# Spectral filter and feed-forward on one core: the inverse transform over d with cosine and sine planes for half of the positions

## The chip, the cores and the metric

The kernel runs on one core of a Trainium2 chip. TensorE (PE in the profile) multiplies, VectorE (DVE) and ScalarE (ACT) work elementwise, GpSimd (POOL) does small things, and SyncE (SP), ACT and POOL issue the transfers (DMA). The metric is the device time of one execution in microseconds; three executions before the change took 1285.08, 1282.17 and 1284.58 us, the median is 1284.58.

## The reference

The input x has 2048 positions of 1024 values. After a layer norm it goes two ways: a two-dimensional real Fourier transform, a pointwise filter and the transform back; and a feed-forward network with 3584 hidden values. Their product is added to x.

```python
xn = _layernorm(x)
X = rfft2(xn, axes=(-2, -1))          # 2048 x 513
s = irfft2(X * (w_r + 1j * w_i), s=(2048, 1024), axes=(-2, -1))
h = silu(einsum("bsd,df->bsf", xn, w1))
g = silu(einsum("bsf,fd->bsd", h, w2))
return x + s * g
```

Only the last step of `irfft2`, the one that goes from 513 frequencies over d to 1024 positions, is touched by the change.

## The kernel before

Every operand of a matmul is split into a high and a low half in float16, and each product is made of three matmuls (high x high, high x low, low x high) that accumulate in float32 in PSUM.

The program is one list of matmuls with other work woven into it. First comes the first layer of the network (`mm1`, tiles pa, line 421), with the layer norm and the forward transform in between. Then comes the second layer: it is computed by seven block products m = 0 to 6 instead of eight (a Strassen scheme over two halves of the rows and of the columns), each with eight row blocks j = 0 to 7 of 42 matmuls of 512 columns (`mm2`, tiles pb, lines 499 to 501). A row block is evacuated by `acc`; its weights `w` are read as `jr`, split by ACT and DVE (lines 216 and 219) in the product before, and its left operands `ht` are loaded on ACT's queue two row blocks ahead (lines 1386 to 1388). Products 4 to 6 also finish output tiles: they read the spectral result back (`fs`) and x (`fx`), multiply, add and store.

The filter (`f_gen`) and the inverse transform (`i_gen`) are background jobs. After every half row block `work` lets them take steps. A meter (lines 175 to 186) adds up an estimated cost for each instruction on PE and on DVE; a background step is taken only while DVE's sum is not more than LEAD = 1.0 ahead of PE's (line 1285). Each job also yields a number of steps of its own.

`i_gen` runs once for each of four column classes c, in the order 1, 3, 0, 2. The four tiles iu (`mat`, line 1121) transform over the positions s; `post` and `split` on ACT and DVE turn them into the operands us, one for each group g of frequencies over d (group 0 holds the residues 0 and 4 modulo 8, group g the residues g and 8 - g). Then for each of four blocks p of 128 rows:

- `mat2(p)` (line 1150) makes one PSUM tile id of four groups x 256 columns. In each group the columns are two planes of 128 positions. It takes 24 matmuls of 256 columns: four groups, three terms, and r = 0 (real part) and 1 (imaginary part). Each has a weight load of 128 x 128 of its own.
- `bfly(p)` copies half of id to SBUF on ACT (line 1156), and on DVE forms sums and differences of groups 0 and 2 and of 1 and 3 (lines 1161 to 1164, 256 elements each), then the eight output pieces of 128 positions with ten operations of 128 elements (lines 1169 to 1178). The tile s is stored to sd by a transfer on SP's queue (line 1189), to be read back as fs.

The PSUM tiles iu and id come from a pool with two buffers (tag ft), the tiles pb from one with four. In SBUF, tags uc, ub, ud and so have one buffer each, s has two. A matmul that writes into a PSUM buffer waits until ACT and DVE have read what was there before; ACT, DVE and each DMA queue take their instructions in the order in which the program issues them.

Of the kernel before, what the change touches and what calls it, by code (L numbers as in the profile page):

```python
# [10 lines left out]
F32 = mybir.dt.float32  # L11
I32 = mybir.dt.int32
AF = mybir.ActivationFunctionType
OP = mybir.AluOpType
# [19 lines left out]
RH = math.sqrt(0.5)  # L34
# [3 lines left out]
def _halves(v, scale):  # L38
    v = v * scale
    hi = v.astype(np.float16)  # L40
    return hi, (v - hi.astype(np.float64)).astype(np.float16)


def make_constants():

    d0 = np.arange(128)[:, None, None]
    d1 = np.arange(8)[None, :, None]
    k1 = np.arange(64)[None, None, :]
    th = 2 * np.pi * (((8 * d0 + d1) * k1) % 1024) / 1024
# [12 lines left out]
    kc = np.stack(_halves(k, 2.0**14), 3)  # L62

    ci = np.zeros((128, 4, 2, 256))
    idx = np.arange(64)[:, None]
    dd = np.arange(128)[None, :]
    alt = np.where(dd[0] % 2 == 0, 1.0, -1.0)
    for g in range(4):
        for h, cl in enumerate((0, 4) if g == 0 else (g, 8 - g)):
            kd = 8 * idx + cl  # L70
            ph = 2 * np.pi * ((kd * dd) % 1024) / 1024
            co, si = 2 * np.cos(ph), 2 * np.sin(ph)
            r = slice(64 * h, 64 * h + 64)
            sg = 1 if h == 0 else -1
            if g == 0:
                ci[r, g, 0] = np.concatenate([co, sg * co], 1)
                ci[r, g, 1] = np.concatenate([-si, -sg * si], 1)
            else:
                ci[r, g, 0] = np.concatenate([co, sg * si], 1)
                ci[r, g, 1] = np.concatenate([-si, sg * co], 1)  # L80
    ci[0, 0, 0] = 1.0
    ci[0, 0, 1] = np.concatenate([alt, alt])
# [12 lines left out]


def spectral_ffn(ctx, tc, x, w_r, w_i, w1, w2, ca, kc, ci, tw, pm, out):
    nc = tc.nc
# [14 lines left out]
    pt = ctx.enter_context(tc.tile_pool(name="pt", bufs=2, space=PSUM))  # L113
# [23 lines left out]
    def defer(n, fn):  # L137
        deferred.append([n, fn])
# [53 lines left out]
    def radix4(sign, b, d, o):  # L192

        sub = nc.vector.tensor_tensor
        plus, minus = ((2, 7), (6, 3)) if sign < 0 else ((6, 3), (2, 7))

        def pick(i):
            st = i[1] - i[0]
            stop = i[1] + (1 if st > 0 else -1)
            return o[:, i[0]:stop:st]  # L200

        sw = d[:, 1, ::-1]
        sub(o[:, 0:2], b[:, 0], b[:, 1], op=OP.add)
        sub(o[:, 4:6], b[:, 0], b[:, 1], op=OP.subtract)
        sub(pick(plus), d[:, 0], sw, op=OP.add)
        sub(pick(minus), d[:, 0], sw, op=OP.subtract)
# [880 lines left out]
    C = {}  # L1087
# [16 lines left out]
    def i_gen(c):  # L1104
        ip = C["p"]
        tt, stt = nc.vector.tensor_tensor, nc.vector.scalar_tensor_tensor
# [17 lines left out]
        def post(g):  # L1124
            ps = psu.pop(g)
            cpy = ip.tile([128, 2, 256], F32, name=f"uc{c}_{g}", tag="uc", bufs=1)
            nc.scalar.activation(cpy, ps[:, 2:4], AF.Copy)
            b = ip.tile([128, 2, 2, 128], F32, name=f"ub{c}_{g}", tag="ub", bufs=1)
            d = ip.tile([128, 2, 2, 128], F32, name=f"ud{c}_{g}", tag="ud", bufs=1)
            tt(b.rearrange("m c r k -> m c (r k)"), ps[:, 0:2], cpy, op=OP.add)  # L1130
            tt(d.rearrange("m c r k -> m c (r k)"), ps[:, 0:2], cpy, op=OP.subtract)
# [11 lines left out]
        psd = {}  # L1143

        def mat2(p):
            ps = pt.tile([128, 2, 2, 256], F32, name=f"id{c}_{p}", tag="ft")
            for g, o in ((0, ps[:, 0, 0]), (2, ps[:, 0, 1]), (1, ps[:, 1, 0]), (3, ps[:, 1, 1])):
                for n, (uh, ch) in enumerate(((0, 0), (0, 1), (1, 0))):
                    for r in range(2):
                        nc.tensor.matmul(o, us[g][:, uh, 2 * p + r], C["ci"][:, ch, g, r], start=(n == 0 and r == 0), stop=(n == 2 and r == 1))  # L1150
            psd[p] = ps

        def bfly(p):
            ps = psd.pop(p)
            cpy = ip.tile([128, 2, 256], F32, name=f"sc{c}_{p}", tag="uc", bufs=1)
            nc.scalar.activation(cpy, ps[:, :, 1], AF.Copy)
            pq = ip.tile([128, 2, 2, 128], F32, name=f"spq{c}_{p}", tag="ub", bufs=1)
            ab = ip.tile([128, 2, 2, 128], F32, name=f"sab{c}_{p}", tag="ud", bufs=1)
            pqf = pq.rearrange("s n r k -> s n (r k)")
            abf = ab.rearrange("s n r k -> s n (r k)")  # L1160
            tt(pqf[:, 0], ps[:, 0, 0], cpy[:, 0], op=OP.add)
            tt(abf[:, 0], ps[:, 1, 0], cpy[:, 1], op=OP.add)
            tt(pqf[:, 1], ps[:, 0, 0], cpy[:, 0], op=OP.subtract)
            tt(abf[:, 1], ps[:, 1, 0], cpy[:, 1], op=OP.subtract)
            pc, qp, pm_, qm = pq[:, 0, 0], pq[:, 0, 1], pq[:, 1, 0], pq[:, 1, 1]
            u, t_, r, v = ab[:, 0, 0], ab[:, 0, 1], ab[:, 1, 0], ab[:, 1, 1]
# [3 lines left out]
            tt(o12[:, 1], r, t_, op=OP.add)  # L1170
            tt(s_[:, 0], pc, u, op=OP.add)
            tt(s_[:, 4], pc, u, op=OP.subtract)
            tt(s_[:, 2], pm_, v, op=OP.subtract)
            tt(s_[:, 6], pm_, v, op=OP.add)
            stt(s_[:, 1], o12[:, 0], RH, qm, op0=OP.mult, op1=OP.add)
            stt(s_[:, 5], o12[:, 0], -RH, qm, op0=OP.mult, op1=OP.add)
            stt(s_[:, 7], o12[:, 1], RH, qp, op0=OP.mult, op1=OP.add)
            stt(s_[:, 3], o12[:, 1], -RH, qp, op0=OP.mult, op1=OP.add)
# [71 lines left out]
    with tc.manual_schedule():  # L1250
# [134 lines left out]
        for n, (m, j) in enumerate(seq):  # L1385
# [15 lines left out]
            ps = pf.tile([128, 512], F32, name=f"pb{m}_{j}", tag="ff")  # L1401
# [52 lines left out]
```

## Time and profile before

| | |
|---|---|
| three timed runs | 1285.08, 1282.17, 1284.58 us |
| span of the profiled execution | 1282.3 us; the page has no other time for this execution |
| PE, DVE, ACT, POOL busy | 1261.7, 951.1, 464.5, 120.1 us |
| id matmuls (line 1150) | 384, first at 934.8, last at 1153.0 us |
| iu matmuls (line 1121) | 384, 43.2 us busy |
| pb matmuls (lines 499 to 501) | 3 x 798, 299.5 to 299.7 us busy for each line |
| read from and written to HBM | 189.06 and 104.33 MB |

A row of the groups reads: line, engine, operation, output <- inputs, shape, count | busy time, mean of one in ns | idle time of the engine just before, and what ended it. A row of the timeline reads: start, duration (us), engine, line, operation, count. A row of the windows reads: the stretch, its length, then busy time and count for PE, weight loads, DVE, ACT and POOL, then the granted clock, the share of the DMA engines and GB/s. A row of the waits reads: who waited <- for whom: total, number, longest.

### The profile page before, as it was taken

The numbers are of one execution on the slowest core, as the hardware profiler recorded it, in microseconds if no ns is written. First come the engines' busy times: TensorE is split into PE (matmuls) and PEld (weight loads), VectorE is DVE, ScalarE is ACT, GpSimd is POOL, SyncE is SP. The second block draws the span as 40 slices with busy tenths as digits, with TensorE's granted clock in tenths as the row PEclk, the third lists the DMA queues.
The fourth block names the chain that finished last, engine by engine and source line by source line (L and its number), as shares of the span: only waits on it lengthen the run. The fifth ranks groups of instructions, "written<-read, shape, count | busy, mean of one in ns | idle before, by whom it ended". The sixth has DMA issues, their size and how long they took to land.

```text
span 1282.3 us, 18847 instructions
## 1 busy us (share of the span) xinstructions
PE 1261.7 (98%) x6991; PEld 656.3 (51%) x6991; DVE 951.1 (74%) x1856; ACT 464.5 (36%) x572; POOL 120.1 (9%) x241
## 2 busy tenths in 40 slices
PE   8999999999999999999999998999999999999997
PEld 5545445444544544445455554544555556564444
DVE  7688988899879897978587998872564657685344
ACT  4864443434455555535242221211322223233111
POOL 2220000002000000012101111132001010000000
PEclk9999999999999999999999998999999999999999
DMA  7585667546676997589789899969597799869894
GB/s 248 131 186 153 167 192 235 168 126 189 215 236 207 288 281 227 171 277 240 184 241 290 216 266 233 280 215 317 127 310 196 277 300 318 288 214 320 267 360 165
DMA packets 267373, 298.86 MB, mean 233 GB/s; under 512 B 38928, under 2 KB 193296, under 8 KB 266640
## 3 DMA queue, kind: packets, MB, share of 16 engines
q1 hardware_dynamic: 247408, 238.85, 62.7%
q10 hardware_dynamic: 15840, 51.45, 11.6%
q0 software_dynamic: 4032, 7.34, 3.5%
q8 instruction: 55, 0.90, 0.3%
q14 instruction: 38, 0.31, 0.1%
HBM read 189.06 MB, written 104.33 MB: 229 GB/s over the span
## 4 chain that ended last, share of the span: by engine, by line
PE 84%; DMA 7%; DVE 4%; SPq 1%; issue 1%; ACT 1%; POOL 0%; ACTq 0%; DVEq 0%; POOLq 0%
PE pa L421 40%; PE pb L499 11%; PE pb L500 11%; PE pb L501 11%; PE id L1150 3%; PE iu L1121 3%; DMA vq<-vd 2%; DMA jr<-ws 1%; SPq L453 1%; PE fx L903 1%; DMA kq<-in_kc_dram 1%; DMA hd_dif<-hoone 1%; ACT xp L658 1%; DMA hd_sum<-hosum 1%; DVE w L219 1%
## 5 line engine op out<-in xcount | busy, mean ns | idle before, releaser
L421 PE MATMUL pa<-xnT,w 128*128 128x512 f16 x2688 | 585.0, 379 | 1.1 <-ACT w L216 0.7
L421 PEld LDWEIGHTS <-w 128*128 128x128 f16 x2688 | 262.1, 98 | 311.9 <-DVE w L219 1.3
L499 PE MATMUL pb<-w,ht 128*128 128x512 f16 (+1 forms) x798 | 299.7, 376 | 0.0
L500 PE MATMUL pb<-w,ht 128*128 128x512 f16 (+1 forms) x798 | 299.5, 375 | 0.0
L501 PE MATMUL pb<-w,ht 128*128 128x512 f16 (+1 forms) x798 | 299.5, 375 | 0.0
L501 PEld LDWEIGHTS <-ht 128*128 128x128 f16 x798 | 78.2, 98 | 91.3 <-issue 0.3
L499 PEld LDWEIGHTS <-ht 128*128 128x128 f16 x798 | 78.2, 98 | 87.9
L500 PEld LDWEIGHTS <-ht 128*128 128x128 f16 x798 | 78.2, 98 | 87.8
L430 ACT ACTIVATE h<-pa,s 128x512 f32<-128x512 f32 x112 | 75.7, 678 | 129.2 <-PE pa L421 117.2
L216 ACT ACTIVATE w<-jr,sc 128x512 f16<-128x512 f32 x98 | 68.4, 713 | 85.6 <-PE pb L501 31.6
L219 DVE SCALAR_TENSOR_TENSOR hoone<-h,hs,hoone 128x2048 f16<-128x2048 f32 x28 | 65.7, 2346 | 18.5 <-ACT hoone L216 18.5
L219 DVE SCALAR_TENSOR_TENSOR w<-jr,sc,w 128x512 f16<-128x512 f32 x98 | 71.7, 749 | 2.0 <-ACT w L216 2.0
L216 ACT ACTIVATE hoone<-h,hs 128x2048 f16<-128x2048 f32 x28 | 55.9, 1998 | 45.3 <-DVE h L464 23.7
L216 ACT ACTIVATE hosum<-hr,hs 128x1536 f16<-128x1536 f32 x28 | 44.0, 1573 | 55.3 <-DVE hr L460 34.3
L930 ACT ACTIVATE zq<-Z,zs 128x1024 f16<-128x1024 f32 x16 | 18.3, 1146 | 104.4 <-DVE Z L1003 57.3
L903 PE MATMUL fx<-vq,kq 128*128 128x256 f16 x192 | 45.5, 281 | 7.8 <-DMA vq<-vd 7.8
L219 DVE SCALAR_TENSOR_TENSOR hosum<-hr,hs,hosum 128x1536 f16<-128x1536 f32 x28 | 50.8, 1814 | 2.5 <-ACT hosum L216 2.5
L459 DVE TENSOR_TENSOR hr<-h 128x1024 f32<-128x1024 f32 x28 | 34.2, 1222 | 21.7 <-ACT h L430 21.5
L216 ACT ACTIVATE w<-w1r,rs 128x1024 f16<-128x1024 f32 x28 | 31.9, 1144 | 47.0 <-DVE w L219 31.8
L580 ACT ACTIVATE pl<-pl,c 128x512 f32<-128x512 f32 (+1 forms) x26 | 16.9, 682 | 82.3 <-DVE pl L559 53.6
L239 DVE TENSOR_REDUCE m<-w1r 128x1 f32<-128x1024 f32 x28 | 33.8, 1211 | 16.1 <-DMA w1r<-in_B_w_dram 16.1
L1150 PE MATMUL id<-cis,us 128*128 128x256 f16 x384 | 43.2, 273 | 0.0
(188 smaller groups left out, 1534.7 us busy)
## 6 DMA issues: line engine op xcount, KB each, us to landing
w1r<-in_B_w_dram SPq DMA_DIRECT2D x28, 512.0 KB, 6.1
hd_sum<-hosum SPq DMA_DIRECT2D x56, 256.0 KB, 2.9
hd_one<-hoone SPq DMA_DIRECT2D x56, 256.0 KB, 3.7
hd_dif<-hoone SPq DMA_DIRECT2D x56, 256.0 KB, 3.2
w2m<-in_B_w_dram SPq DMA_DIRECT2D x28, 512.0 KB, 5.4
ht<-hd_dif ACTq DMA_DIRECT2D x32, 448.0 KB, 8.3
jr<-in_B_w_dram SPq DMA_DIRECT2D x56, 256.0 KB, 6.1
ht<-hd_sum ACTq DMA_DIRECT2D x32, 448.0 KB, 5.3
```

Of the source, the lines that this page charges most:

```text
L216: nc.scalar.activation(hi, raw, AF.Copy, scale=scale)
L219: nc.vector.scalar_tensor_tensor(lo, raw, scale, hi, op0=OP.mult, op1=OP.subtract)
L239: nc.vector.tensor_reduce(m1[:, i:i + 1], raw[i], axis=AX.XY, op=OP.max, apply_absolute_value=True)
L421: nc.tensor.matmul(ps, w[:, wh, d], xt[:, xh, d], start=(n == 0), stop=(n == 23))
L430: nc.scalar.activation(hq[:, 2 * (c % 2) + f % 2], ps, AF.Silu, scale=s1[:, f:f + 1])
L459: tt(sums[:, 0:2], hq[:, 0::2], hq[:, 1::2], op=OP.subtract)
L499: nc.tensor.matmul(ps, hh[:, 0], w[:, 0], start=first, stop=False)
L500: nc.tensor.matmul(ps, hh[:, 0], w[:, 1], start=False, stop=False)
L501: nc.tensor.matmul(ps, hh[:, 1], w[:, 0], start=False, stop=last)
L903: nc.tensor.matmul(o, k[:, c, kh, 1], v[:, c, vh], start=(n == 0), stop=False)
L1121: nc.tensor.matmul(ps[:, q], lhs, rhs, start=(n == 0 and r == 0), stop=(n == 2 and r == 1))
L1150: nc.tensor.matmul(o, us[g][:, uh, 2 * p + r], C["ci"][:, ch, g, r], start=(n == 0 and r == 0), stop=(n == 2 and r == 1))
```

## The change

A cosine is the same at positions d and 128 - d, a sine has the opposite sign. The constants ci no longer hold two full planes of 128 positions, but for each plane the positions below 64 in order or 63 down to 1, the cosines (r = 0, columns 0 to 129) apart from the sines (r = 1, columns 127 or 130 to 255). Columns 127 to 129 hold the positions 64 and 0 that have no partner. `mat2` keeps its 24 matmuls for a tile, but those of r = 0 have 130 columns, those of r = 1 have 129 in groups 1 to 3 and 256 in group 0; the groups now follow in the order 0, 1, 2, 3. In `bfly`, ACT copies the sine columns (504 elements) and two sets of 8 single positions; DVE forms near - sine and near + sine for 63 positions of every plane (two operations of 504 elements, the second written backwards), then sums and differences of groups 0 and 2, 1 and 3 (two operations of 512), and the same ten operations of 128 with outputs in two runs of 64. The tile pa is new; dm takes the buffer of the copy (uc), o12 a part of kk (ub). In `post`, the tiles b and d become one tile.

```diff
-    dd = np.arange(128)[None, :]
+    dd = np.arange(65)[None, :]
+    up, down = slice(1, 64), slice(63, 0, -1)
...
+            re, im = ci[r, g, 0], ci[r, g, 1]
+            re[:, 0:64], re[:, 127] = co[:, 0:64], co[:, 64]
+            im[:, 127], im[:, 130:193] = si[:, 64], si[:, up]
             if g == 0:
-                ci[r, g, 0] = np.concatenate([co, sg * co], 1)
-                ci[r, g, 1] = np.concatenate([-si, -sg * si], 1)
+                re[:, 64:127], re[:, 128], re[:, 129] = sg * co[:, down], sg * co[:, 64], sg * co[:, 0]
+                im[:, 128], im[:, 193:256] = sg * si[:, 64], -sg * si[:, down]
             else:
-                ci[r, g, 0] = np.concatenate([co, sg * si], 1)
-                ci[r, g, 1] = np.concatenate([-si, sg * co], 1)
+                re[:, 64:127], re[:, 128] = sg * si[:, down], sg * si[:, 64]
+                im[:, 128], im[:, 129], im[:, 193:256] = -sg * co[:, 64], sg * co[:, 0], sg * co[:, down]
...
         def mat2(p):
-            ps = pt.tile([128, 2, 2, 256], F32, name=f"id{c}_{p}", tag="ft")
-            for g, o in ((0, ps[:, 0, 0]), (2, ps[:, 0, 1]), (1, ps[:, 1, 0]), (3, ps[:, 1, 1])):
-                for n, (uh, ch) in enumerate(((0, 0), (0, 1), (1, 0))):
-                    for r in range(2):
-                        nc.tensor.matmul(o, us[g][:, uh, 2 * p + r], C["ci"][:, ch, g, r], start=(n == 0 and r == 0), stop=(n == 2 and r == 1))
+            ps = pt.tile([128, 4, 256], F32, name=f"id{c}_{p}", tag="ft")
+            for g in range(4):
+                for r, cols in enumerate((slice(0, 130), slice(0 if g == 0 else 127, 256))):
+                    for n, (uh, ch) in enumerate(((0, 0), (0, 1), (1, 0))):
+                        nc.tensor.matmul(
+                            ps[:, g, cols], us[g][:, uh, 2 * p + r], C["ci"][:, ch, g, r, cols],
+                            start=(r == 0 and n == 0), stop=(r == 1 and n == 2), skip_group_check=True)
...
         def bfly(p):
-            cpy = ip.tile([128, 2, 256], F32, name=f"sc{c}_{p}", tag="uc", bufs=1)
-            nc.scalar.activation(cpy, ps[:, :, 1], AF.Copy)
-            pq = ip.tile([128, 2, 2, 128], F32, name=f"spq{c}_{p}", tag="ub", bufs=1)
-            ab = ip.tile([128, 2, 2, 128], F32, name=f"sab{c}_{p}", tag="ud", bufs=1)
...
-            tt(pqf[:, 0], ps[:, 0, 0], cpy[:, 0], op=OP.add)
-            tt(abf[:, 0], ps[:, 1, 0], cpy[:, 1], op=OP.add)
-            tt(pqf[:, 1], ps[:, 0, 0], cpy[:, 0], op=OP.subtract)
-            tt(abf[:, 1], ps[:, 1, 0], cpy[:, 1], op=OP.subtract)
+            cpy = ip.tile([128, 4, 2, 63], F32, name=f"sc{c}_{p}", tag="uc", bufs=1)
+            kk = ip.tile([128, 4, 4, 64], F32, name=f"sk{c}_{p}", tag="ub", bufs=1)
+            nc.scalar.activation(cpy.rearrange("s g k d -> s g (k d)"), ps[:, :, 130:256], AF.Copy)
+            nc.scalar.activation(kk[:, :, 0:2, 0], ps[:, :, 0:128:127], AF.Copy)
+            nc.scalar.activation(kk[:, :, 2:4, 0], ps[:, :, 129:127:-1], AF.Copy)
+            near = ps[:, :, 1:127].rearrange("s g (k d) -> s g k d", k=2)
+            tt(kk[:, :, 0::3, 1:64], near, cpy, op=OP.subtract)
+            tt(kk[:, :, 1:3, 63:0:-1], near, cpy, op=OP.add)
+            pa = ip.tile([128, 2, 2, 128], F32, name=f"spa{c}_{p}", tag="pa", bufs=1)
+            dm = ip.tile([128, 2, 2, 128], F32, name=f"sdm{c}_{p}", tag="uc", bufs=1)
+            tt(pa.rearrange("s g k d -> s (g k d)"), kf[:, 0:512], kf[:, 512:1024], op=OP.add)
+            tt(dm.rearrange("s g k d -> s (g k d)"), kf[:, 0:512], kf[:, 512:1024], op=OP.subtract)
...
-            o12 = ip.tile([128, 2, 128], F32, name=f"so{c}_{p}", tag="so", bufs=1)
+            o12 = kf[:, 0:256].rearrange("s (n d) -> s n d", n=2)
...
-            tt(s_[:, 0], pc, u, op=OP.add)
+            tt(both(0), pair(pc), pair(u), op=OP.add)
...
-            stt(s_[:, 1], o12[:, 0], RH, qm, op0=OP.mult, op1=OP.add)
+            stt(both(1), pair(o12[:, 0]), RH, pair(qm), op0=OP.mult, op1=OP.add)
...
```

`both(j)` is the pair of runs of 64 positions, first the run 2j and then the run 15 - 2j, of the sixteen in the tile s; `pair` cuts an operand into two runs of 64.

More of the change, by code (lines that the diff above doesn't have):

```diff
@@ L65, in make_constants @@
     idx = np.arange(64)[:, None]
-    dd = np.arange(128)[None, :]
-    alt = np.where(dd[0] % 2 == 0, 1.0, -1.0)
+    dd = np.arange(65)[None, :]
+    up, down = slice(1, 64), slice(63, 0, -1)
     for g in range(4):
@@ L74, in make_constants @@
             sg = 1 if h == 0 else -1
+            re, im = ci[r, g, 0], ci[r, g, 1]
+            re[:, 0:64], re[:, 127] = co[:, 0:64], co[:, 64]
+            im[:, 127], im[:, 130:193] = si[:, 64], si[:, up]
             if g == 0:
-                ci[r, g, 0] = np.concatenate([co, sg * co], 1)
-                ci[r, g, 1] = np.concatenate([-si, -sg * si], 1)
-            else:
-                ci[r, g, 0] = np.concatenate([co, sg * si], 1)
-                ci[r, g, 1] = np.concatenate([-si, sg * co], 1)
-    ci[0, 0, 0] = 1.0
-    ci[0, 0, 1] = np.concatenate([alt, alt])
+                re[:, 64:127], re[:, 128], re[:, 129] = sg * co[:, down], sg * co[:, 64], sg * co[:, 0]
+                im[:, 128], im[:, 193:256] = sg * si[:, 64], -sg * si[:, down]
+            else:
+                re[:, 64:127], re[:, 128] = sg * si[:, down], sg * si[:, 64]
+                im[:, 128], im[:, 129], im[:, 193:256] = -sg * co[:, 64], sg * co[:, 0], sg * co[:, down]
+    alt = np.where(np.arange(64) % 2 == 0, 1.0, -1.0)
+    ci[0, 0, 0, 0:130] = 1.0
+    ci[0, 0, 1, 0:64], ci[0, 0, 1, 64:127], ci[0, 0, 1, 127:130] = alt, alt[down], 1.0
     ci = np.stack(_halves(ci, 2.0**13), 1)
@@ L1127, in post @@
             nc.scalar.activation(cpy, ps[:, 2:4], AF.Copy)
-            b = ip.tile([128, 2, 2, 128], F32, name=f"ub{c}_{g}", tag="ub", bufs=1)
-            d = ip.tile([128, 2, 2, 128], F32, name=f"ud{c}_{g}", tag="ud", bufs=1)
+            bd = ip.tile([128, 2, 2, 2, 128], F32, name=f"ub{c}_{g}", tag="ub", bufs=1)
+            b, d = bd[:, 0], bd[:, 1]
             tt(b.rearrange("m c r k -> m c (r k)"), ps[:, 0:2], cpy, op=OP.add)
@@ new lines, in bfly @@
+            pa = ip.tile([128, 2, 2, 128], F32, name=f"spa{c}_{p}", tag="pa", bufs=1)
+            dm = ip.tile([128, 2, 2, 128], F32, name=f"sdm{c}_{p}", tag="uc", bufs=1)
+            kf = kk.rearrange("s g k d -> s (g k d)")
+            tt(pa.rearrange("s g k d -> s (g k d)"), kf[:, 0:512], kf[:, 512:1024], op=OP.add)
+            tt(dm.rearrange("s g k d -> s (g k d)"), kf[:, 0:512], kf[:, 512:1024], op=OP.subtract)
+            pc, qp, u, t_ = pa[:, 0, 0], pa[:, 0, 1], pa[:, 1, 0], pa[:, 1, 1]
@@ new lines, in bfly, with both @@
+            pm_, qm, r, v = dm[:, 0, 0], dm[:, 0, 1], dm[:, 1, 0], dm[:, 1, 1]
+            o12 = kf[:, 0:256].rearrange("s (n d) -> s n d", n=2)
+            s_ = ip.tile([128, 8, 128], F32, name=f"s{c}_{p}", tag="s", bufs=2)
+            sides = s_.rearrange("s a (h d) -> s (a h) d", h=2)
+            def both(j):
+                first, other = 2 * j, 15 - 2 * j
+                step = other - first
+                stop = other + (1 if step > 0 else -1)
+                return sides[:, first:(None if stop < 0 else stop):step]
@@ L1169, in bfly, with pair @@
+            def pair(a):
+                return a.rearrange("s (h d) -> s h d", h=2)
             tt(o12[:, 0], r, t_, op=OP.subtract)
             tt(o12[:, 1], r, t_, op=OP.add)
[L1171 to L1174, printed above, removed]
-            stt(s_[:, 1], o12[:, 0], RH, qm, op0=OP.mult, op1=OP.add)
-            stt(s_[:, 5], o12[:, 0], -RH, qm, op0=OP.mult, op1=OP.add)
@@ L1177, in bfly @@
-            stt(s_[:, 7], o12[:, 1], RH, qp, op0=OP.mult, op1=OP.add)
-            stt(s_[:, 3], o12[:, 1], -RH, qp, op0=OP.mult, op1=OP.add)
+            tt(both(0), pair(pc), pair(u), op=OP.add)
+            tt(both(4), pair(pc), pair(u), op=OP.subtract)
+            tt(both(2), pair(pm_), pair(v), op=OP.subtract)
+            tt(both(6), pair(pm_), pair(v), op=OP.add)
+            stt(both(1), pair(o12[:, 0]), RH, pair(qm), op0=OP.mult, op1=OP.add)
+            stt(both(5), pair(o12[:, 0]), -RH, pair(qm), op0=OP.mult, op1=OP.add)
@@ L1179, in bfly @@
+            stt(both(7), pair(o12[:, 1]), RH, pair(qp), op0=OP.mult, op1=OP.add)
+            stt(both(3), pair(o12[:, 1]), -RH, pair(qp), op0=OP.mult, op1=OP.add)
             sf = s_.rearrange("s a b -> s (a b)")
```

4 lines of the change are left out of this document (removed).

## The prediction

> **What bounds the kernel now.** I read the totals first, then the chain that ended last, the idle time of PE by stretches, and last the order of time around the changed matmuls.
>
> ```profile
> span 1282.3 us, 18847 instructions
> PE 1261.7 (98%) x6991; PEld 656.3 (51%) x6991; DVE 951.1 (74%) x1856; ACT 464.5 (36%) x572; POOL 120.1 (9%) x241
> PE 84%; DMA 7%; DVE 4%; SPq 1%; issue 1%; ACT 1%; POOL 0%; ACTq 0%; DVEq 0%; POOLq 0%
> L1150 PE MATMUL id<-cis,us 128*128 128x256 f16 x384 | 43.2, 273 | 0.0
> ...
> core 0: us, PE busy (x) PEld busy (x) DVE busy (x) ACT busy (x) POOL busy (x), PEclk, DMA share, GB/s
> ...
> 1175.00:1190.00 15.00, 15.00 (x71) 6.82 (x70) 6.73 (x10) 4.47 (x7) 0.00 (x0) 1.00 0.80 267
> 1212.00:1221.00 9.00, 9.00 (x44) 4.08 (x42) 4.08 (x6) 1.33 (x2) 0.00 (x0) 1.00 1.00 345
> 1221.00:1230.00 9.00, 9.00 (x44) 4.05 (x43) 4.08 (x6) 1.33 (x2) 0.00 (x0) 1.00 1.06 393
> 1117.00:1266.00 149.00, 149.00 (x754) 73.55 (x752) 80.15 (x158) 33.65 (x52) 0.00 (x0) 1.00 0.84 283
> 906.00:1153.00 247.00, 247.00 (x1525) 149.03 (x1524) 160.73 (x392) 66.47 (x98) 19.00 (x22) 1.00 0.80 254
> ```
>
> The whole inverse transform lies in the stretch from 906 to 1153 us. There PE is busy for 247.00 of 247.00 us at granted clock 1.00, DVE for 161, ACT for 66. The 384 matmuls of line 1150 have no idle time before them (last column 0.0), and nothing in this stretch makes PE wait. So a microsecond taken from PE's instructions here moves everything behind it forward, unless the change makes a wait that PE does not have today. The sum below is therefore PE time first and then a look at each thing that could become late.
>
> **What a matmul of mat2 costs now, and what a narrow one costs.** A busy mean (273 ns) overlaps with the next instruction; the cost of one in a stream is the distance of starts.
>
> ```profile
> 947.15 2.78 PE L1150 MATMUL id<-cis,us 128*128 128x256 f16 x24
> 949.77 0.38 PE L499 MATMUL pb<-w,ht 128*128 128x512 f16 x1
> 949.99 0.38 PE L500 MATMUL pb<-w,ht 128*128 128x512 f16 x1
> ...
> 335.12 0.22 PE L731 MATMUL fa<-cas,xnT 128*128 128x128 f16 x1
> ...
> 336.41 0.22 PE L733 MATMUL fa<-cas,xnT 128*128 128x128 f16 x1
> 336.46 10.52 PE L421 MATMUL pa<-xnT,w 128*128 128x512 f16 x48
> ...
> L1150 PEld LDWEIGHTS <-us 128*128 128x128 f16 x384 | 37.6, 98 | 6.1
> ```
>
> 24 matmuls of 256 columns take 949.77 - 947.15 = 2.62 us, 109.2 ns each, so all 384 take 41.9 us. The forward transform has the narrow case already: the 24 matmuls of one fa tile, 128 columns each and each with a weight load of its own, take 336.46 - 335.12 = 1.34 us, 55.8 ns each. The line through the two points is 0.417 ns a column: 56.7 ns for 130 columns, 56.3 ns for 129.
>
> **The change on PE.** For each of the 16 (c, p) the 24 matmuls stay 24, and so do their weight loads. 12 of them (r = 0) now have 130 columns, 9 (r = 1, groups 1 to 3) have 129, and 3 (r = 1, group 0) keep 256: 12 x 56.7 + 9 x 56.3 + 3 x 109.2 = 1515 ns, against 24 x 109.2 = 2621 ns. That is 1.106 us less for each, **17.7 us in all**.
>
> Two things here have no row. The 129-column matmuls begin at column 127, an odd start for the operand and for the output; no matmul of this trace does. Between 56.3 ns (the fa row) and 109.2 ns (no gain at all from being narrow) the 144 of them cost 0 to 144 x 53 ns = 7.6 us more. I take 0: length and types are those of the fa row. The other is the weight load, 98 ns by its own row and longer than 56 ns. The fa rows have the same load before every matmul and still start every 56 ns, so I take it as hidden; unhidden at 98 ns each, 336 narrow matmuls would cost 32.9 us instead of 19.0 us, 13.9 us more.
>
> The Trainium skill speaks against the change at this place: "TensorE: Matmul & The Clock Gate", section "Back-to-back issue gap", gives about 81 ns for a matmul of 128 columns in a stream of pairs of load and matmul. By that figure the 336 would cost 27.2 us (an estimate), and the saving would be 9.5 us, a time of about 1275 us. The fa rows, the same stream of pairs in this kernel, disagree with it at 55.8 ns, and the sum goes by them. As a mechanism it is the unhidden load among the rivals.
>
> **The change on ACT and DVE.** These prices come from the starts of consecutive instructions.
>
> ```profile
> 981.07 0.68 DVE L1131 TENSOR_TENSOR ud<-iu,uc 128x512 f32<-128x512 f32 x1
> 981.67 0.41 DVE L203 TENSOR_TENSOR uu<-ub 128x256 f32<-128x256 f32 x1
> 982.00 0.42 DVE L204 TENSOR_TENSOR uu<-ub 128x256 f32<-128x256 f32 x1
> ...
> 943.60 0.28 DVE L1170 TENSOR_TENSOR so<-sab 128x128 f32<-128x128 f32 x1
> 943.80 0.28 DVE L1171 TENSOR_TENSOR s<-spq,sab 128x128 f32<-128x128 f32 x1
> ...
> L1156 ACT ACTIVATE sc<-id 128x512 f32<-128x512 f32 x16 | 9.6, 597 | 56.3 <-PE id L1150 30.3 <-DVE so L1170 14.0 <-DVE sab L1164 11.9
> L1299 ACT ACTIVATE warm<-ones 128x1 f32<-128x1 f32 x1 | 0.2, 203 | 0.0
> ...
> L786 DVE TENSOR_TENSOR V<-EO 128x65 f32<-128x65 f32 x16 | 3.6, 222 | 0.0
> L784 DVE TENSOR_TENSOR V<-EE 128x63 f32<-128x63 f32 x16 | 3.5, 219 | 0.0
> L1003 DVE TENSOR_TENSOR Z<-yb 128x128 f32<-128x128 f32 x32 | 13.4, 459 | 0.0
> ...
> DVE spq L1161 <- ACT sc L1156: 22.3, 6, 8.3
> ```
>
> Today bfly takes four operations of 256 elements (0.33 us apart) and ten of 128 (0.20 us apart): 3.3 us. After it, two operations of 504 elements that form positions d and 128 - d, two of 512 (0.60 us apart), and the same ten: 4.4 us, 1.1 us more, 17 us over 16 calls. Reversed writes are not dearer in themselves: line 784 writes 63 elements backwards in 219 ns, line 786 writes 65 forwards in 222 ns. ACT gets two copies of 8 elements more for each call, near the 203 ns of the one-element row: 6.5 us in all. I cost both engines at **nothing**: the cover is PE's own work, 247 us against 161 + 17 on DVE and 66 + 7 on ACT. Without that cover it would be the 17 us of DVE, all of the gain.
>
> New waits: cpy and dm share one buffer, and o12 lies in kk, so ACT's copies for p + 1 wait until DVE has finished bfly(p); before, they waited for the first four operations only. Behind them on ACT's queue stand the evacuation of a pb tile, a weight split, and two ht loads. The pb tiles have four buffers of one row block each. An ht load is issued two row blocks ahead, 2 x 42 x 0.216 us (949.99 - 949.77) = 18 us.
>
> ```profile
> DMA to landing us min/median/max: 3.3/6.4/16.6
> ...
> zt<-zd SPq DMA_DIRECT2D x4, 2048.0 KB, 9.0
> sd<-s SPq DMA_DIRECT2D x16, 512.0 KB, 4.6
> kk<-in_kc_dram SPq DMA_DIRECT2D x4, 768.0 KB, 12.3
> ```
>
> At the median landing of ht (first row), 6.4 us, about 11.7 us are left for a hold of at most one bfly, 4.4 us. Only the slowest landing, 16.6 us, would leak, some 3 us once. I take 0.
>
> PE itself waits for PSUM: id_2 needs id_0's buffer back, id_3 needs id_1's. The instruction listing of the changed kernel shows id_0 and id_1 together, then half a row block of pb (21 matmuls, 4.5 us), id_2, another half, id_3 (before: id_0 to id_2 together, half a block, id_3). The planner counts less PE time and more DVE time for each step, so it spreads them. With id_0 starting at 0, it ends at 1.5; ACT needs 1.0 and DVE's two PSUM reads 1.2, so the buffer is free at 3.7 and wanted at 7.5. bfly(0) with a weight split (0.67 us) ends at 7.6, ACT's next copies and DVE's next reads at 9.8; id_3 wants that at 13.5. Both have 3.7 us to spare, if DVE is not late when id_0 ends. It is not today: the waits row shows DVE waiting for the first copy for up to 8.3 us.
>
> The same listing moves the later stages back: the last id tile goes from row block 2 of product 5 to the end of that product, 8 row blocks before the end. The last call of bfly falls into product 6, and its rows are wanted only from its row block 4. No load or store appears or vanishes on SP's queue; stores of s (512 KB each) and the loads of zt and kk (2048 and 768 KB) shift behind other transfers there. A store of s that waits on SP for its bfly holds the jr, pd and fs transfers behind it, as it does today; jr is split in the product before the one that needs it, so I take 0 for that too, and the volume is a rival below.
>
> **Sum.** 1282.3 - 17.7 = 1264.6 us of span. The median of the three runs, 1284.58, lies 2.3 above that span, which I keep: **1266.9 us**. The runs spread by 2.9 us.
>
> **The rivals.**
>
> *The odd start costs.* Nothing in the trace speaks for it but the lack of a row. In full it gives 1266.9 + 7.6 = 1274.5 us.
>
> *The load is no longer hidden.* For it: 98 ns against 56. Against it: the fa rows, which differ from the new ones by one or two columns. It gives 1266.9 + 13.9 = 1280.8 us.
>
> *The chain of ACT and DVE paces the id stage.* Every call waits for the one before it: 1.0 on ACT and 4.4 on DVE, 5.4 us a call, 21.6 a stage, while PE needs 4 x 1.5 + 2 x 4.5 = 15.1. The strided row Z (459 ns for 128 elements against 284, 1.62 times) is for it. At that ratio on every operation of bfly the need of id_3 is met at 1.5 + 1.0 + 7.1 + 0.67 + 1.0 + 1.9 = 13.2, still before 13.5; from there it decides, and at twice the count (8.8 and 2.4) it is met at 15.4: 1.9 us lost in each of four stages, 1274.5 us. The reversed rows at par are against it.
>
> *The transfers become the bound, and it gets slower.* The stores of s for c = 0 (four of 512 KB) and the loads of zt and kk for c = 2 (2.9 MB) move into the last two products, 1117 to 1266 now. These carry 283 GB/s x 149 us = 42.2 MB; 47 MB in the same PE time asks for 317 GB/s. From there down it costs; below 47 / (149 + 17.7) = 282 GB/s nothing of the gain is left; at the 267 GB/s of the stretch from 1175 to 1190 it takes 176 us, 27 us late, and 1266.9 + 27 = 1294 us. Against it: 345 and 393 GB/s in two stretches of product 6, so 267 looks like what was asked for rather than a limit.
>
> **How the numbers follow.** Forecast 0.80; odd start 0.07; unhidden load 0.03; paced by the chain 0.03; transfers 0.07, of which 0.05 end slower than before and 0.02 within the measurement's reach. A measurement tells about 0.2%, 2.6 us, from no change. The first four all end faster by more than that: faster 0.93, same 0.02, slower 0.05. The range runs from 1263.5 (the forecast less the spread of the runs) to 1275.5 (the odd start in full with 1 us of spread), which holds the first two cases.
>
> **What would show it.** In the profile after, PE's busy time should fall by about 17 us and its idle time stay. The starts of the narrow id matmuls should be 56 to 57 ns apart; 107 for those with 129 columns alone is the odd start, 80 to 98 for all narrow ones the load. DVE should gain about 17 us and ACT about 6. Waits of PE for a DVE operation on id, between id_1 and id_3, would show the chain; idle PE in products 5 and 6 that ends with ht or w would show the transfers. The prediction is wrong if PE's share of the chain that ended last is filled by anything but PE between the first iu and the last pb.

## The result and the profile after

The changed kernel took 1269.99 us (median of four runs, 1267.74 to 1271.87), the kernel before 1283.51 us beside it (four runs, 1282.17 to 1285.08): a ratio of 0.989, 95% interval 0.9868 to 0.9912. The forecast was 1266.9 us. The profiled execution of the changed kernel is the run of 1267.74 us, its span 1266.0 us.

The totals of the page after, and the group that has idle time before it where it had none (last column: idle time, and what ended it):

```profile
span 1266.0 us, 18895 instructions
...
PE 1243.7 (98%) x6991; PEld 641.7 (51%) x6991; DVE 969.0 (77%) x1856; ACT 466.9 (37%) x604; POOL 120.1 (9%) x241
...
PE 79%; DMA 9%; DVE 8%; ACT 2%; issue 1%; SPq 1%; POOL 0%; ACTq 0%; DVEq 0%; POOLq 0%
...
L1125 PE MATMUL iu<-kk,zt 128*128 128x256 f16 x384 | 43.2, 273 | 1.2 <-DVE zt L1115 1.2
```

The same group before:

```profile
L1121 PE MATMUL iu<-kk,zt 128*128 128x256 f16 x384 | 43.2, 273 | 0.0
```

PE is busy 18.0 us less than before (1261.7), DVE 17.9 us more (951.1). There is a wait that was not there, 1.2 us before an iu tile. PE's share of the chain falls from 84% to 79%, which is far more than 1.2 us, because the chain follows that wait back through what led to it: from 984 to 1063 us it holds no work of PE, though PE is idle in them for 1.2 us only. Before the change the chain stays on PE from the first iu to the last pb.

The PE timeline of one stage after, around the tiles id (start, duration, engine, line, operation, count; a run of matmuls is shown under the shape of its first):

```profile
934.79 3.22 PE L1154 MATMUL id<-cis,us 128*128 128x130 f16 x48
937.84 0.38 PE L503 MATMUL pb<-w,ht 128*128 128x512 f16 x1
...
942.37 1.69 PE L1154 MATMUL id<-cis,us 128*128 128x130 f16 x24
943.90 0.38 PE L503 MATMUL pb<-w,ht 128*128 128x512 f16 x1
```

Two tiles take 937.84 - 934.79 = 3.05 us, a single one 1.53 us. A stage of four takes 3.05 + 1.53 + 1.53 = 6.11 us; before it took 4 x 2.62 = 10.48. That is 4.37 us a stage, 17.5 us in four. No PE idle time stands before any of these matmuls.

The operations of the new `bfly`, in the groups between 880 and 1160 us (12 of the 16 calls; us busy, mean ns, idle before):

```profile
L1172 DVE TENSOR_TENSOR spa<-sk 128x512 f32<-128x512 f32 x12 | 8.3, 692 | 0.4
L1173 DVE TENSOR_TENSOR sdm<-sk 128x512 f32<-128x512 f32 x12 | 8.2, 685 | 0.0
L1167 DVE TENSOR_TENSOR sk<-id,sc 128x504 f32<-128x504 f32 x12 | 8.1, 678 | 14.9 <-ACT sk L1165 14.8
L1168 DVE TENSOR_TENSOR sk<-id,sc 128x504 f32<-128x504 f32 x12 | 8.1, 672 | 0.0
...
L1165 ACT ACTIVATE sk<-id 128x8 f32<-128x8 f32 x12 | 2.3, 190 | 0.0
L1164 ACT ACTIVATE sk<-id 128x8 f32<-128x8 f32 x12 | 2.1, 178 | 0.0
```

The new operations cost what the sum of the prediction took, the backward write (line 1168) no more than the forward one. ACT is busy only 2.4 us more in all (464.5 to 466.9).

**Where the 1.2 us are.** The timeline after, around PE's wait (in brackets the idle time of the engine, and who ended it):

```profile
1061.38 0.72 ACT L220 ACTIVATE w<-jr,sc 128x512 f16<-128x512 f32 x1 [7.90 <-DMA jr<-in_B_w_dram]
...
1062.14 0.75 DVE L223 SCALAR_TENSOR_TENSOR w<-jr,sc,w 128x512 f16<-128x512 f32 x1 [3.33 <-ACT w L220]
...
1062.81 0.20 DVE L1115 COPY zt<-zp 128x16 f16<-128x16 f16 x1
...
1063.07 1.70 PE L1125 MATMUL iu<-kk,zt 128*128 128x256 f16 x14 [1.18 <-DVE zt L1115]
```

The first iu tile of c = 0 needs a copy of 16 elements on DVE. The load of its tile was issued at 997 us and lands after 9 to 12 us, so its data are there, but on DVE's queue it stands behind the second half of a weight split, which waits for ACT's half, which waits 7.9 us for its weight block jr. The chain that ended last shows what jr came behind, in order of time (start, us, what; the profile infers these steps):

```profile
1024.62 7.34 DMA ht<-hd_one
...
1031.98 10.49 DMA fs<-sd
...
1043.44 9.47 DMA jr<-in_B_w_dram
...
1053.47 7.89 DMA jr<-in_B_w_dram
```

The same 52 us in the windows, first of after, then of before (columns as in the prediction; the last two are the share of the DMA engines and GB/s):

```profile
1010.00:1062.00 52.00, 51.89 (x309) 26.50 (x306) 36.33 (x83) 11.77 (x25) 6.05 (x7) 1.00 1.02 334
```

```profile
1010.00:1062.00 52.00, 52.00 (x318) 30.92 (x317) 34.91 (x93) 12.86 (x19) 6.04 (x7) 1.00 0.90 279
```

In this stretch the transfers carry 334 GB/s instead of 279, and the share of the DMA engines is 1.02 instead of 0.90. The waits of ACT for jr between 1000 and 1110 us (total, number, longest), after and before:

```profile
ACT w L220 <- DMA jr<-in_B_w_dram: 20.0, 6, 7.9
```

```profile
ACT w L216 <- DMA jr<-in_B_w_dram: 3.0, 1, 3.0
```

So the spans add up: 1282.3 - 17.5 + 1.2 = 1266.0 us.

### The profile page after: what moved, and what is told of

It reads as the page before. It is cut to its first block, busy times and chain, and to the rows that moved or that the text cites. A ratio compares the mean times of both kernels' runs of the same rounds, so it can differ in the third digit from the quotient of the medians.

```text
span 1266.0 us, 18895 instructions
## 1 busy us (share of the span) xinstructions
PE 1243.7 (98%) x6991; PEld 641.7 (51%) x6991; DVE 969.0 (77%) x1856; ACT 466.9 (37%) x604; POOL 120.1 (9%) x241
## 4 chain that ended last, share of the span: by engine, by line
PE 79%; DMA 9%; DVE 8%; ACT 2%; issue 1%; SPq 1%; POOL 0%; ACTq 0%; DVEq 0%; POOLq 0%
PE pa L425 37%; PE pb L505 11%; PE pb L503 11%; PE pb L504 11%; DMA vq<-vd 3%; PE iu L1125 3%; PE fx L907 2%; PE id L1154 1%; DMA jr<-in_B_w_dram 1%; DMA ht<-hd_one 1%; DMA fs<-sd 1%; PE fx L909 1%; PE fx L908 1%; ACT xp L662 1%; DMA zd<-zq 1%
## 5 line engine op out<-in xcount | busy, mean ns | idle before, releaser
L243 DVE TENSOR_REDUCE m<-w1r 128x1 f32<-128x1024 f32 x28 | 33.8, 1212 | 16.3 <-DMA w1r<-in_B_w_dram 16.3
L1125 PE MATMUL iu<-kk,zt 128*128 128x256 f16 x384 | 43.2, 273 | 1.2 <-DVE zt L1115 1.2
```

The lines of the kernel that those rows point to most:

```text
L243: nc.vector.tensor_reduce(m1[:, i:i + 1], raw[i], axis=AX.XY, op=OP.max, apply_absolute_value=True)
L1125: nc.tensor.matmul(ps[:, q], lhs, rhs, start=(n == 0 and r == 0), stop=(n == 2 and r == 1))
```

## The experiments

The theory after this: PE's saving is whole, and a late zt copy behind late weights gives about a microsecond of it back. The rivals: the three microseconds that the median, 1269.99, lies above the forecast belong to the id stage (the chain of ACT and DVE), to DVE's and ACT's added work, or to the scatter of the runs.

**The changed kernel once more** (no edit).

> The changed kernel once more, for a second trace and more times. Theory A (late vector work in product 4): in the first trace PE has one new idle gap, 1.2 us before the iu tiles of c = 0, where the copy into zt on DVE stands behind weight splits whose jr transfers are late; the three other runs are 1 to 4 us longer than the profiled one because this gap varies. A expects this trace to show the same gap, 1 to 5 us, and its time to follow it: about 1266.5 plus the gap. Theory B (the gap is all there is, the other runs vary elsewhere): time 1268 to 1272 whatever the gap is, and idle time of PE ahead of 900 us that is larger than the 20 us or so of the traces before.

Measured: 1268.69 us (five runs, 1263.1 to 1270.68), ratio 0.9874 [0.9856, 0.9891]. In this trace PE waits only 0.24 us before that iu tile, and the span is 1261.3 us. The wait is the same in place and not in size; the runs scatter over 7.6 us.

**Earlier start of a stage.** `i_gen` lets four steps of other work pass before each later stage; here two.

```diff
-            for _ in range(4):
+            for _ in range(2):
                 yield PAUSE
```

> The changed kernel, but each inverse transform after the first skips 2 pauses instead of 4 before it starts, which puts the iu tiles of c = 0 at row block 3 of product 4, as before the change, and leaves the order inside each id stage as it is now. Theory A (the place of the stage costs): the gap of PE before iu of c = 0 is gone and the whole saving of PE time shows, 17.7 us under the median of before: 1265.5 to 1266.5. Theory B: as the changed kernel, 1269 to 1271. A third way, that zt is now wanted before its load has landed, would show as an idle PE that ends with the zt copy or with the zt load, and more than 1271.

Measured: 1265.11 us (four runs, 1264.54 to 1266.36), 0.9854 [0.9841, 0.9867]. No idle PE from 800 us to the last matmul. ACT's wait for jr, between 1000 and 1110 us, is there and short:

```profile
ACT w L220 <- DMA jr<-in_B_w_dram: 6.4, 2, 4.7
```

**The copy alone earlier.** The zt copy goes to DVE two steps sooner, everything else stays.

```diff
-            for _ in range(4):
+            for n in range(4):
+                if n == 2:
+                    nc.vector.tensor_copy(C["z"][c][:, :, :, :, 0, 0], zp[:, c])
                 yield PAUSE
...
-        nc.vector.tensor_copy(zt[:, :, :, :, 0, 0], zp[:, c])
+        if c == IORDER[0]:
+            nc.vector.tensor_copy(zt[:, :, :, :, 0, 0], zp[:, c])
```

> The changed kernel with the DVE copy into zt issued two pauses (one row block) earlier, ahead of the weight splits that hold it; the order of the matmuls is unchanged. Theory A: no idle PE before iu of c = 0, 1265.5 to 1267. Theory B: 1269 to 1271, since the other runs' time is elsewhere. If the gap then ends with another DVE or ACT operation of post, DVE as a whole is late there, not the copy alone.

Measured: 1268.79 us (six runs, 1265.72 to 1273.96), 0.988 [0.986, 0.99]. The wait is not gone; it moved into the stage, to the third iu tile, which needs a PSUM buffer that DVE has not yet read (waits of PE):

```profile
PE iu L1128 <- DVE ub L1138: 2.3, 1, 2.3
```

DVE is late there because ACT is (timeline of the same trace):

```profile
1068.23 0.72 ACT L220 ACTIVATE w<-jr,sc 128x512 f16<-128x512 f32 x1 [3.54 <-DMA jr<-in_B_w_dram]
1068.86 0.58 ACT L1134 ACTIVATE uc<-iu 128x512 f32<-128x512 f32 x1
...
1069.47 0.69 DVE L1137 TENSOR_TENSOR ub<-iu,uc 128x512 f32<-128x512 f32 x1 [4.60 <-ACT uc L1134]
```

So it is not the copy alone. Late weights hold ACT's queue as they hold DVE's, and the next small operation behind a split is the one that makes PE wait. This trace shows a second price. PE's timeline around the wait, then three windows of the same trace (third figure from the right: the granted clock):

```profile
1065.74 2.78 PE L1128 MATMUL iu<-kk,zt 128*128 128x256 f16 x24
1070.82 4.46 PE L1128 MATMUL iu<-kk,zt 128*128 128x256 f16 x24 [2.29 <-DVE ub L1138]
1075.11 0.38 PE L503 MATMUL pb<-w,ht 128*128 128x512 f16 x1
```

```profile
1067.80:1071.20 3.40, 1.11 (x11) 0.75 (x10) 1.73 (x4) 1.21 (x2) 0.00 (x0) 1.00 1.08 327
1071.20:1074.60 3.40, 3.40 (x19) 2.45 (x17) 2.28 (x5) 2.15 (x3) 0.00 (x0) 0.50 1.00 318
1074.60:1078.00 3.40, 3.40 (x20) 1.78 (x19) 3.37 (x8) 0.99 (x2) 0.00 (x0) 0.99 0.95 368
```

The tile after the wait takes 1075.11 - 1070.82 = 4.29 us where its like takes 2.62: after a pause of 2.29 us the granted clock is 0.50 for 3.4 us, and that costs 1.7 us more. The pause of 1.18 us in the trace of after is followed by clock 1.00.

**The stages at their old places.** The planner counts the old cost for the tiles and for `bfly`, so that the tiles stand at the places of before.

```diff
+            clock["pe"] += 0.4215e-3 * (24 * 256 - (12 * 130 + 9 * 129 + 3 * 256))
             psd[p] = ps
...
             ps = psd.pop(p)
+            clock["dve"] -= 1.05e-3 * (2 * 504 + 2 * 512 - 4 * 256)
```

> The changed kernel with the meter given the old costs of mat2 and bfly, so that every matmul stands where it stood before the change: id_0, id_1 and id_2 follow each other without a half row block between. Theory A: no gap before iu of c = 0, but id_2 now wants its PSUM buffer 3.0 us after id_0 starts and has it at 3.7, and id_3 just in time: 0.7 us of idle PE in each of four stages, 2.8 us, all of it ending with DVE's reads of id; 1268 to 1269. If the later placement was free and its spreading of id needed nothing, 1270; if the waits at id_2 are absent, 1266.

Measured: 1273.24 us (four runs, 1271.83 to 1273.78), 0.9914 [0.9902, 0.9927], slower than the changed kernel. The waits of PE:

```profile
PE iu L1125 <- DVE zt L1115: 4.2, 2, 3.2
PE id L1154 <- DVE sk L1170: 3.0, 4, 0.8
```

With three tiles in a row, id_2 waits about 0.76 us for its buffer in each of the four stages: the spreading by the planner, on which the prediction's 3.7 us to spare rested, is needed. And the late zt is not made by the late places alone; here two stages have it, and the longer pause, 3.2 us, is again followed by 3.4 us at clock 0.50. The chain of the earlier of these two stages begins with the last operation of a bfly:

```profile
955.04 0.21 DVE s L1200
...
955.27 0.32 SPq L1211
...
955.69 7.30 DMA jr<-in_B_w_dram
...
963.55 6.79 DMA jr<-in_B_w_dram
...
970.36 0.73 ACT w L220
...
971.79 0.21 DVE zt L1115
```

SP's queue holds the store of s (line 1211) until its bfly is done, and the load of jr stands behind that store. In the other stage, at 1091 us, a load of pl stands there in the place of jr. The prediction had named this hold and taken it for nothing.

**The new bfly without the narrow matmuls.** All id matmuls keep 256 columns, at the places of before; ACT's and DVE's part is the new one.

```diff
-                for r, cols in enumerate((slice(0, 130), slice(0 if g == 0 else 127, 256))):
+                for r, cols in enumerate((slice(0, 256), slice(0, 256))):
...
+            clock["dve"] -= 1.05e-3 * (2 * 504 + 2 * 512 - 4 * 256)
```

> ACT's and DVE's part alone: the new constants, bfly and buffers, but every matmul of mat2 takes all 256 columns (the unused constants are zero), and the meter gets the old costs, so that every matmul stands and lasts as before the change. The prediction costed this part at nothing: 1282 to 1285, the time of before. Theory C: DVE's 17 us more are not all covered; up to 1287. With 2.6 us for each of three tiles, id_2 wants its buffer at 5.2 and has it at 4.8, so no idle PE at id; a gap before iu as with the old places (4 us in all there) is possible where the transfers are late: 1284 to 1288 then.

Measured: 1284.39 us (twelve runs), 1.0002 [0.999, 1.0013]. The totals of its page:

```profile
PE 1261.6 (98%) x6991; PEld 655.8 (51%) x6991; DVE 969.5 (76%) x1856; ACT 466.0 (36%) x604; POOL 119.8 (9%) x241
```

DVE has the whole addition and the time is that of before: with PE's work as long as it was, the addition costs nothing.

**The narrow matmuls without the new bfly.** The kernel before, with the new constants and the narrow `mat2` (old cost in the planner). This kernel leaves out the sums and differences of positions d and 128 - d. Of the edit, the loops and constants of the change are not printed again:

```diff
-            ps = pt.tile([128, 2, 2, 256], F32, name=f"id{c}_{p}", tag="ft")
+            ps = pt.tile([128, 4, 256], F32, name=f"id{c}_{p}", tag="ft")
...
+            clock["pe"] += 0.4215e-3 * (24 * 256 - (12 * 130 + 9 * 129 + 3 * 256))
```

> PE's part alone: the new constants and the narrow matmuls in their new order, followed by the bfly of before (the output is not the reference's: the sums of positions d and 128 - d are not formed), the meter with the old cost of mat2, so that every matmul stands where it stood. Prediction: 17.7 us less on PE. With the bfly of before id_0's buffer is free at 1.5 + 0.6 + 1.3 = 3.4 and wanted at 3.05, 0.35 us of idle PE in each of four stages: 1283.6 - 17.7 + 1.4 = 1267.3; no more than that if the rest of the loss with the old places (4 us before iu) comes from the longer bfly, 1271 if it comes from the transfers in the shorter time.

Measured: 1268.64 us (four runs, 1267.52 to 1270.15), 0.9882 [0.9865, 0.9898]. Here too PE waits for buffers, longer for each than the 0.35 us expected:

```profile
PE id L1154 <- DVE sab L1171: 2.7, 4, 0.7
PE iu L1125 <- DVE zt L1115: 0.4, 1, 0.4
```

The stages at their old places differ from this run by the new bfly with its buffers, and they took 1273.24 us, 4.6 us more (intervals of the ratios 0.9902 to 0.9927 and 0.9865 to 0.9898). There the waits for zt came to 4.2 us, here to 0.4. So the new bfly is free beside the wide matmuls, and not beside the narrow ones at these places; it is the later places, with the tiles spread, that hide most of it.

**The later places without the change.** The kernel before, with the planner counting the costs of the changed one:

```diff
+            clock["pe"] -= 0.4215e-3 * (24 * 256 - (12 * 130 + 9 * 129 + 3 * 256))
             psd[p] = ps
...
             ps = psd.pop(p)
+            clock["dve"] += 1.05e-3 * (2 * 504 + 2 * 512 - 4 * 256)
```

> The kernel before with the meter given the new costs, so that every matmul stands where the change puts it (last id tile at the end of product 5), with the old matmuls and the old bfly. Theory A: the late place alone makes the transfers of product 4 late; a gap before iu of c = 0 of 0 to 3 us, 1283.5 to 1286.5, and ACT's waits for jr between 1010 and 1120 us of 10 us or more (3 us before). If it takes the shorter PE time too to make them late: 1283.5, no gap, and waits for jr as before.

Measured: 1283.42 us (twelve runs), 1.0001 [0.9989, 1.0012], and no wait of PE, although ACT waits for jr as in after (between 1000 and 1110 us):

```profile
ACT w L216 <- DMA jr<-in_B_w_dram: 18.5, 2, 10.0
```

The places cost nothing by themselves. Here the zt copy of c = 0 starts at 1066.84 us and PE comes to that iu at 1069.86, so the lateness of the weights stops 2.8 us short of PE. In the changed kernel the copy starts 4.0 us earlier, at 1062.81, but PE is ready 8.0 us earlier, at 1061.89. The late weights reach PE there because PE's own work has become shorter and what feeds the stage has not kept up with it; DVE's longer work may have a part in that, which this run does not separate.

**Less to transfer.** This kernel leaves out the sums of two weight blocks, which accumulating transfers form.

```diff
-SUMMED = (4, 5)
+SUMMED = ()
```

> The changed kernel without the second block that POOL adds into jr in products 4 and 5: 28 accumulating transfers of 256 KB are left out, so the sums of two weight blocks are not formed; every matmul and every ACT and DVE instruction stays where it is. Theory A (in products 4 and 5 the transfers are late, ACT's weight split waits for jr, and DVE's queue with the zt copy and post waits behind it): no idle PE before or inside iu of c = 0, ACT's waits for jr shrink from about 20 us in the stretch from 1000 to 1110 us to a few, and the time is 1264 to 1266 with a spread under 2 us, as with fewer pauses. Theory C (DVE is late from its own amount of work after the change): gap and spread stay, 1268 to 1270.

Measured: 1265.17 us (four runs, 1264.14 to 1266.39), 0.9854 [0.9838, 0.9871]. Its window of the 52 us:

```profile
1010.00:1062.00 52.00, 52.00 (x302) 26.86 (x300) 37.12 (x85) 12.46 (x27) 0.00 (x0) 1.00 0.94 338
```

PE has no wait behind 800 us, ACT none for jr between 1000 and 1110 us (9.4 us for fs instead), and the zt copy of c = 0 starts at 1054.36 us, 4.9 us ahead of its iu. The DMA share is 0.94 at 338 GB/s, as many GB/s as after. What is missing are the 28 transfers that add a second block to a first (POOL's row falls from 241 to 213 instructions); the rate alone does not make the weights late. ACT's and DVE's work is that of the changed kernel, so DVE's amount of work alone does not make the wait either.

**More lead for these sums**, one block earlier:

```diff
-            join(n + 2)
+            join(n + 3)
```

> The changed kernel with POOL's adding transfer issued three weight pieces ahead of its split instead of two; nothing else moves. If jr is late because the add has too little lead: ACT's waits for jr in products 4 and 5 shrink, no idle PE at iu of c = 0, 1264.5 to 1266.5 with a spread under 2 us, like the kernels with fewer pauses and without the sums. If jr is late because the volume in this stretch (1.02 of the transfer engines, 334 GB/s) is at its limit, the add only waits for its first half instead: 1268 to 1270, a gap as now.

Measured: 1269.08 us (four runs, 1265.73 to 1271.09), 0.988 [0.9863, 0.9896]. The lead was not what was missing: ACT waits 8.4 us for jr instead of 20.0, but 6.7 us each for ht and fs in their place, and PE's wait stays:

```profile
PE iu L1125 <- DVE zt L1115: 1.3, 1, 1.3
```

**One step instead of four** (`range(1)` in the edit of the earlier start).

> Fewer pauses taken further: 1 instead of 4 (2 gave 1265.11), each transform starts half a row block to one block earlier still. If the place only has to be ahead of the crowded stretch, 1264.5 to 1266, as with 2. If zt is wanted before its load has landed, idle PE that ends with the zt copy, 1267 or more. It cannot be below 1264 by theory A, since with 2 pauses no PE is idle behind 800 us any more.

Measured: 1267.12 us (four runs, 1266.16 to 1271.03), 0.9865 [0.9845, 0.9884]. Now the wait stands 39 us later, before the last stage, 1.7 us. In this trace an earlier start moves the wait and does not end it.

**Changed kernel and two steps again, side by side** (no new edit).

> The changed kernel a third time, beside fewer pauses on the same chip. Open: the two traces so far have gaps of 1.2 and 0.24 us before iu of c = 0 (time from the first iu to the end 359.8 and 358.8 us), while the nine times spread from 1263.1 to 1271.9. If the place of the stage is what costs, its median is 2 us or more above that of fewer pauses here too, and the stretch from the first iu to the end is 359 to 363 us. If the stretch ahead of the first iu, which the change does not touch (902.5 to 907.6 us in the traces), is what varies, the two kernels differ by less than 1 us.

> The kernel with 2 pauses again, beside the changed one on the same chip. If the place costs: from the first iu to the end 358.6 us again, no idle PE there, spread under 3 us, 2 to 4 us under the changed kernel. If not: the same median as the changed kernel within 1 us.

Measured: 1266.53 us (four runs, 1264.54 to 1267.39), 0.9863 [0.9847, 0.988] for the changed kernel; 1266.55 us (four runs, 1265.92 to 1268.51), 0.9869 [0.9849, 0.9888] with two steps. PE's wait is 1.7 us in the one trace and 0.3 in the other, and the times are equal. Over all runs the medians are 1267.74 us for the changed kernel (13 runs), 1266.14 with two steps (8 runs) and 1283.86 before (52 runs). Two steps take away a wait that the traces show; that the kernel is faster for it is not shown.

**Where the rest of the scatter is.** The changed operations begin with the first iu, and from there to the end of the span the traces differ as their waits do: before 376.15 us, after 359.8, third trace 360.35, the repeated run 358.8, two steps 358.6. Less 17.5 and plus the wait, 376.15 gives 359.85, 360.35, 358.9 and 358.65. The stretch ahead of it, which the change does not touch, runs from 902.45 to 907.57 us in the traces. There PE waits for vq in the filter, and the clock answers or does not. The PE timeline and two windows of after:

```profile
782.79 0.37 PE L907 MATMUL fx<-vq,kq 128*128 128x256 f16 x1 [5.70 <-DMA vq<-vd]
```

```profile
777.00:782.80 5.80, 0.10 (x2) 0.04 (x2) 5.80 (x13) 1.15 (x1) 0.00 (x0) 0.79 0.96 363
782.80:787.00 4.20, 4.20 (x30) 3.54 (x31) 4.20 (x6) 1.33 (x2) 0.00 (x0) 0.50 0.95 212
```

and of the repeated run:

```profile
781.19 0.27 PE L907 MATMUL fx<-vq,kq 128*128 128x256 f16 x1 [3.97 <-DMA vq<-vd]
```

```profile
777.00:781.30 4.30, 0.33 (x3) 0.13 (x2) 4.30 (x9) 0.59 (x1) 0.00 (x0) 1.00 0.93 345
781.30:787.00 5.70, 5.70 (x51) 3.88 (x50) 5.47 (x8) 1.33 (x2) 0.66 (x2) 1.00 0.93 184
```

After 5.70 us of waiting the matmuls run at clock 0.50, after 3.97 us at 1.00. The first iu starts at 906.18 us in the one and at 902.49 in the other.

## Why the prediction was right, and which term was not

- **What bounds the kernel**: right. PE's busy time fell by 18.0 us and the span by 16.3, so PE is idle 1.7 us more. The last sign that the prediction gave for being wrong did come: the chain is filled by other engines from 984 to 1063 us. What that cost PE is the 1.2 us above.
- **PE's term**: 17.7 us forecast, 17.5 measured in the stages. The odd start costs nothing: 48 matmuls take 3.05 us, the sum gave 2 x 1.515 = 3.03. The weight load stays hidden: less the six wide matmuls at 109.2 ns, the 42 narrow ones are 57 ns apart. By the 81 ns of the Trainium skill ("TensorE: Matmul & The Clock Gate", section "Back-to-back issue gap") the 42 narrow ones of these 48 alone would take 3.4 us (an estimate), so the trace disagrees with it here too.
- **DVE and ACT at nothing**: right for the changed kernel, but not for the first reason given, that PE's 247 us cover 178 on DVE. The totals were the same with the tiles at their old places, and there the new bfly cost 4.6 us beside the narrow matmuls. It cost nothing beside the wide ones (1.0002). DVE's 17 us came as 17.9. ACT's 6.5 us came as 2.4: the small copies have the 178 to 190 ns of their rows, but overlap with their neighbours.
- **The waits in the id stage**: right. No PE wait stands between id_0 and id_3; with the old order there is one of 0.76 us a stage, so the argument by the spread order was the one that mattered. The strided writes kept to the reversed row (672 ns against 678), not to Z's.
- **The zero that was wrong**: "jr is split in the product before the one that needs it, so I take 0 for that too". The weights do come in time for PE. What the step missed is who stands behind them: the late split delays the small work behind it, on DVE's queue (the zt copy) or on ACT's (uc, in the early copy), that lets the next iu go on. It measured 0.2 to 1.7 us in three traces of the changed kernel; in two edited kernels, where it came to 2.3 and 3.2 us, the halved clock took 1.7 and 1.6 us more (in the second, 72 iu matmuls took 9.66 us instead of 8.04).
- **The transfers as a rival**: the mechanism is real, its place was wrong (product 4, where sums of weights, fs, ht and the moved zt and kk meet, not the last two), and it costs about a microsecond of the gain, not all of it. The last two products of the changed kernel, 1092 to 1262 us, carry 288 GB/s, 49 MB where 47 were forecast. By the prediction's sum, in which 282 GB/s leave nothing of the gain and 317 all of it, most of the gain would be lost at that rate; yet PE waits nowhere in them. The sum set the larger volume against the old 149 us, but the matmuls of the moved stages came along with their transfers, and the stretch is longer.
- **From span to time**: 1264.6 + 2.3 was forecast, 1266.0 + 1.74 was that of the profiled run; the 2.3 compared a span with a median of other executions. The 2.25 us from there to the first median, 1269.99, are not traced. Over all 13 runs the median is 1267.74, 0.8 above the forecast, which is less than two runs of one kernel differ by: a hit that close is luck, the range is not. Whether the slower ones of these runs had a longer wait at the iu stage, clock included, or only a longer one in the filter, stays open.

## What to carry to other kernels

Where one engine is busy all the time, price a narrower instruction by the distance of starts in the nearest row of the same stream, and pay for it with work on engines that are covered. Test both halves alone, and do not add up the two results: the shorter work of the busy engine is itself a part of the cover, and totals of busy time do not show where it ends. Then list what stands on the same in-order queue ahead of the small instruction that releases the busy engine, because in these traces a late transfer reached it there and not where its data are used. A short wait can still be one after which the clock is halved: here a pause of 2.29 us cost about 4 us, and those of 1.7 us only themselves.

## What the runs showed of the hardware

- The granted clock was 0.50 for 3.4 us around the end of pauses of 2.29 us (early copy) and 3.2 us (old places), and for 6.8 us with one of 5.70 us (filter), where it fell during the pause; it stayed at 1.00 with one of 3.97 us. The Trainium skill ("TensorE: Matmul & The Clock Gate", section "What's actually happening") has a free-running window of some 3.4 us that has to be idle. The length agrees; but the pause of 2.29 us is shorter than such a window, and the 3.40 us ahead of the drop in that trace had PE busy for 1.11, so an idle window in the strict sense was not needed.
- Matmuls of 129 columns that begin at an odd column, with float32 output at an odd start, cost the same as aligned ones (48 matmuls in 3.05 us, 3.03 by the aligned rows).
